# Top k of the first four units inside the weight rounding, first units no longer hurried, four chunks of 128 tokens, kept scores made in steps 4 to 11

## The chip, the cores and the metric

The kernel runs on one core of a Trainium2 chip. The metric is the device time of one execution in microseconds. Three runs of the kernel before gave 1446.69, 1447.28 and 1449.47 us; the median is 1447.28 us.

A core has a matrix engine (PE in the profile, with its weight loads as PEld), a vector engine (DVE), a scalar engine (ACT), GpSimd (POOL) and a queue engine (SP) that here issues nearly all DMA transfers. The program gives each its own list of instructions in a fixed order, with semaphore waits between the lists.

## The reference

Attention that keeps the 32 largest scores of each query, then a two-layer block with leaky ReLU. In NumPy, cut to what is computed:

```python
# q, k, v: (8 batches, 8 heads, 576, 64) float32
scores = 0.125 * q @ k.transpose(0, 1, 3, 2)
kth = np.partition(scores, -32, axis=-1)[..., -32:-31]
scores = np.where(scores >= kth, scores, -1e9)
attn = np.exp(scores - scores.max(-1)); attn /= attn.sum(-1) + 1e-9
x = (attn @ v).transpose(0, 2, 1, 3).reshape(4608, 512)
h = x @ w_in                       # w_in  (512, 2048)
out = np.maximum(0.01 * h, h) @ w_out   # w_out (2048, 512)
```

The two weights arrive as float64 (the scaling by `1/sqrt(...)` in the setup makes them so), and the kernel rounds them to float32 on the chip.

## The kernel before, in words

**Units and steps.** The heads are taken in pairs. A *unit* is 128 query rows of one head pair: a tile of scores of 128 x (2 x 576). There are 144 units, in the order batch, then block of 128 queries, then the four head pairs. One unit is one *step* of the main loop, which takes two steps per turn: `even(s)` (L801) and `odd(s)` (L858). A unit passes through:

- scores on PE (`scores`, L235), copied to `s_sb` by ACT (`keep_scores_of`, L244), two steps ahead of its own step;
- top k on DVE in its step (`top_k`): two `pairs` operations of max and min of the halves (L308), then four rounds of MAX8 (L314) and three of MATCH_REPLACE8 (L319) for each of the two heads;
- in the next step `limits` (ACT L329, POOL L330 and L331), `mask` (ACT L335), `exponents` (ACT L338) and `sums` (ACT L343, tile `ze`);
- `reciprocals` on DVE (L347, tile `rz` from `ze`), then `normalize` on ACT (L350);
- the transpose of the weights into `wT`. The usual way is `split` (two POOL copies L359, each written to DRAM from SP, L360) and `transpose` (a DMA transpose from SP, L364). For the units named in `HASTY` (L673) it is `transpose_in_haste` (PE L374) and `keep_transposed` (ACT L380), a step earlier;
- the product with v (`weigh_whole`, PE L403), copied into a chunk of `x` (`keep_values`, ACT L426). `values_at(n)` (L675) says at which step: three after the pair's second step, two for units in haste.

**The dense block.** Tokens are gathered into chunks (`CHUNKS`, L54), two of 128 and then 17 of 256. The first `EARLY` chunks go through `plain` (L629: `hidden_of_few`, PE L443 with ACT L438, transposes L460 with ACT L462, and PE L634); the others through `mlp` with a scheme of seven products (PE L542 and L556, ACT L530, sums on POOL in L481). `sum_weights` (L493) makes sums of the second weight on POOL, and `sum_last_weights` (L504) two more at the first chunk of the second kind. A chunk becomes ready when all its units are weighed (`ready_at`). Its matmuls are dealt out in slots, seven per step: `mlp_steps(budget)` issues matmuls until `budget` columns are used, and `slot_budget` (L701) gives `EARLY_SHARE` columns per slot while no more than `EARLY` chunks have become ready; later it spreads what is ready evenly up to the next chunk. Copies that follow a group of matmuls are put off to the next `catch_up()`.

**Kept scores.** The scores of twelve later units are made in the first steps (`score_early`, with the count per call from `EARLY_SCORES`, L682) by `keep_scores`: PE L288, ACT L292, then a DMA to DRAM (L294). They are fetched back before those units.

**The start.** Before the main loop the weights are loaded in 16 pieces of 1 MB and rounded in 17 jobs (the first piece in two halves). One job of `round_weights` is a POOL copy (L131), three short DVE operations (L132 to L134), three ACT operations (L135, L137, L139), six matmul steps (L149 to L151), and, after a `yield`, two DVE operations (L153, L156). The second part of a job is issued after the first part of the next one. The raw pieces use three buffers, so piece p is loaded into the buffer of piece p-3 when its job has read it (`load_weights`, L111). The main loop starts when the last job has been issued.

**Order.** All of this is an order written by hand; the tile framework adds the semaphore waits and the rotation of buffers (`bufs`), no reordering.

Of the kernel before, what the change touches and what calls it, by code (L numbers as in the profile page):

```python
# [16 lines left out]
NKC = 5  # L17
# [3 lines left out]
def kernel(  # L21
# [29 lines left out]
    WCH = 1024  # L51
    LEFT = S % P
    assert D == 64 and S == 576 and HP == 4 and B % 2 == 0 and LEFT == 64
    CHUNKS = [128] * 2 + [256] * 17  # L54
    assert sum(CHUNKS) == B * S
    CHMAX = max(CHUNKS)
    LOADED, LOADED_V = 7, 5
# [39 lines left out]
        return w_out[f // 4][:, f % 4:f % 4 + 2, :].rearrange("p g n -> p (g n)")  # L97

    raw_of = {}

    def load_weights(n):
        if n >= NPIECE:
# [12 lines left out]
    def round_weights(n, c0, c1):  # L115

        raw = raw_of[n][:, c0:c1, :]
        dst = piece(n)[:, c0:c1]
        wide = c1 - c0
        mid = raw[:, :, 2]
        low = raw_of[n].rearrange("p n w -> p (n w)").bitcast(U32).rearrange("p (n w) -> p n w", w=2)[:, c0:c1, 0]
        top = raws.tile([P, WCH], U16, name="top", bufs=2)[:, 0:wide]
        scale = raws.tile([P, WCH], U16, name="scale", bufs=2)[:, 0:wide]
        parts = work.tile([P, 2 * NKC - 1, P], F32, name="wT", bufs=3)
        parts = parts.rearrange("p c n -> p (c n)").bitcast(U16)
        m_top, m_low = parts[:, 0:wide], parts[:, WCH:WCH + wide].bitcast(BF16)  # L130
        nc.gpsimd.tensor_copy(top, raw[:, :, 3])  # L131
        nc.vector.tensor_scalar(scale, top, 4, 0x7FF, ALU.logical_shift_right, ALU.bitwise_and)  # L132
        nc.vector.tensor_scalar(m_top, top, 0xF, 0x3F80, ALU.bitwise_and, ALU.bitwise_or)
        nc.vector.tensor_scalar(top, top, 0x8000, None, ALU.bitwise_and)  # L134
        nc.scalar.activation(dst, mid, AF.Copy, bias=-7.0 - 2.0 ** -16, scale=2.0 ** -20)  # L135

        nc.scalar.activation(m_low, low, AF.Copy, bias=128.0, scale=2.0 ** -29)  # L137

        nc.scalar.activation(scale.bitcast(BF16), scale, AF.Exp, bias=least, scale=LN2)  # L139
        if n < NPIECE - 4 or n % 2 == 0:  # L140
            tag, bufs = ("wide", 2) if n < NPIECE - 4 else ("narrow", 1)
            pw = ps_sc.tile([P, 2, 512], F32, name=tag, bufs=bufs)
            sums = [(pw[:, c // 512, :], c) for c in range(0, wide, 512)]
            ends = [(pw.rearrange("p h n -> p (h n)")[:, 0:wide], 0)]
        else:
            ends = sums = [(ps_ml.tile([P, 512], F32, name="pw", tag="ml"), h * 512) for h in range(2)]
        for pw, c in sums:
            at = slice(c, c + 512)
            nc.tensor.matmul(pw, ident_top, m_top[:, at].bitcast(BF16), start=True, stop=False)  # L149
            nc.tensor.matmul(pw, ident, dst[:, at], start=False, stop=False)  # L150
            nc.tensor.matmul(pw, ident_low, m_low[:, at], start=False, stop=True)  # L151
        yield
        nc.vector.tensor_tensor(scale, scale, top, ALU.bitwise_or)  # L153
        for pw, c in ends:
            at = slice(c, c + pw.shape[-1])
            nc.vector.tensor_tensor(dst[:, at], pw, scale[:, at].bitcast(BF16), ALU.mult)  # L156
# [122 lines left out]
    def keep_scores(u):  # L279
# [5 lines left out]
        for half in range(2):  # L285
            for i, _, side, _ in u.parts:
                d = slice(side * D, (side + 1) * D)
                nc.tensor.matmul(ps[i][:, half, 0:HS], qt[d, :], kt[d, half * HS:(half + 1) * HS],  # L288
                                 start=True, stop=True)
        both = gT.rearrange("p f n -> p (f n)")[:, k % 3 * 2 * S:(k % 3 + 1) * 2 * S]  # L290
        for i in range(2):
            nc.scalar.copy(both[:, i * S:(i + 1) * S].rearrange("p (h n) -> p h n", h=2), ps[i][:, :, 0:HS])  # L292
        kept_of[u] = kept.tile([P, 2 * S], F32, name=f"kept{k}")
        nc.sync.dma_start(kept_of[u], both)  # L294

    def fetch_scores(u):
        u.both = work.tile([P, 2, S], F32, name="s_sb", bufs=5)
# [130 lines left out]
    QUARTERS = NKC  # L428
    FULL = list(range(NKC - 1))

    EARLY = 2

    def hidden_of_few(ch, x):

# [235 lines left out]

    HASTY = (*range(4), 14, 15, 142, 143)  # L673

    def values_at(n):  # L675

# [2 lines left out]
    steps = units  # L679

    KEPT = (26, 62, 98)
    EARLY_SCORES = {0: 4, 1: 2, 2: 2, 3: 2, 4: 2}  # L682

    def unit(n):
        return steps[n] if 0 <= n < len(steps) else None

    done_tokens, ready_at = [0] * len(CHUNKS), []
    for n, u in enumerate(steps):
        ch, _ = x_at(u.b * S + u.q0)
        done_tokens[ch] += u.rows * len(u.pairs)  # L690
        if done_tokens[ch] == CHUNKS[ch] * HP:
            ready_at.append(((values_at(n) | 1), ch))
    assert [ch for _, ch in ready_at] == list(range(len(CHUNKS)))

    def attended(s):
# [11 lines left out]
        group = [GROUP * (at % 2 == 0 and at < len(steps)) for at in range(s, until)]  # L707
        return max((backlog[0] + sum(group)) / len(group) - group[0], 0.0) / SLOTS

    EARLY_SHARE = 500  # L710
    GROUP = 1400
    SLOTS = 7

    with tc.manual_schedule():
# [39 lines left out]
                    break  # L754


        for n in range(3):
            load_weights(n)
        jobs = [round_weights(*job) for job in ROUNDED] if AS_WORDS else [iter(())] * len(ROUNDED)
        for n in range(len(jobs) + 1):  # L760
            if n == len(jobs) - 1:
                first = first_scores(steps[0])
                next(first, None)
            for job in jobs[max(n - 1, 0):n + 1][::-1]:
                next(job, None)
            if n == len(jobs) - 1:
                next(first, None)
                load_v(0)
                load_v(1)
            elif n == len(jobs):  # L770
                for _ in first_scores(steps[1]):
                    pass
            if n:
                load_weights(n + 2)
            if n >= len(jobs) - 2 and to_load:
                load_early(to_load.pop(0))
            if 0 <= n - len(jobs) + HP + 1 < HP:
                load_qk(n - len(jobs) + HP + 1)

        def values(s, spare):  # L780
            weighed = []
            for n in range(0, len(steps), 2):
                if values_at(n) != s:
                    continue
                us = steps[n:n + 2]
                po = spare.pop(0) if spare else ps_sc.tile([P, 2, 512], F32, name="wide", bufs=2)
                if len(us[0].pairs) == 1:
                    weigh_whole(us, po, FULL + [QUARTERS])
                    weighed.append((us[0], po[:, :, 0:P]))
                    continue  # L790
                for k, u in enumerate(us):
                    part = po[:, :, k * LEFT:(k + 1) * LEFT]
                    weigh_left(u, part)
                    weighed.append((u, part))
            return weighed

        def keep(weighed):
# [3 lines left out]
        def even(s):  # L801
# [28 lines left out]
            if old:  # L830
                exponents(old, 0)
                exponents(old, 1)
                sums(old)
            if older and in_haste:
                keep_transposed(older)
            if old:
# [6 lines left out]
                normalize(old, 0)  # L843
                normalize(old, 1)
            sum_now(2)
            score_early(EARLY_SCORES.get(s, 0))
            mlp_steps(budget)
            mlp_steps(budget)
            if unit(s + 3) in early_units:
# [8 lines left out]
        def odd(s, new, ps, weighed):  # L858
# [25 lines left out]
                keep(values(s, []))  # L884
            attended(s)
            budget = slot_budget(s)
            if s == 7:
                sum_weights()
            sum_now(3)
            mlp_steps(budget)  # L890
# [4 lines left out]
            if old and not in_haste:  # L895
                exponents(old, 1)
                sums(old)
            for _ in range(4):
                mlp_steps(budget)
            if unit(s + 3) in early_units:  # L900
                fetch_scores(unit(s + 3))
            score_early(EARLY_SCORES.get(s, 0))
            load_more(s)

        for s in range(0, len(steps) + 4, 2):
            assert s < 5 or not to_keep
            odd(s + 1, *even(s))
        mlp_steps(1e9)
        sum_now()
# [61 lines left out]
```

## Time and profile before

| | |
|---|---|
| median of three runs | 1447.28 us |
| the profiled execution: its time, and its span | 1447.51 us, 1445.7 us |
| DVE busy | 1318.6 us (91% of the span) |
| PE busy | 1363.7 us (94%) |
| ACT busy | 1028.6 us (71%) |
| POOL busy | 712.5 us (49%) |
| first `pairs` operation of unit 0, 4, 28 | 60.56, 95.79, 340.20 us |
| first `pairs` operation of the last unit, 143 | 1356.56 us |
| granted TensorE clock, mean | 0.976 |

How to read it: times are from the start of the profiled span. A row of a timeline or a group has line, engine, operation, output and inputs, shapes; "idle before" is time for which the engine stood still, with what ended it. The chain of waits follows the work back from the last instruction; idle time of an engine that is not on it costs nothing. The profiled execution's time is 1.8 us above its span (what lies around the program).

### The profile page before, as it was taken

How to read it: one execution, taken by the hardware profiler on the slowest of the kernel's cores; microseconds unless marked ns; L12 is line 12 of the kernel's file. 1: busy time of each engine (PE TensorE's matmuls, PEld its weight loads, DVE VectorE, ACT ScalarE, POOL GpSimd, SP SyncE). 2: the span in 40 equal slices, each digit the busy share in tenths (PEclk: the TensorE clock that was granted, in tenths of full speed). 3: DMA queues.
4: the chain of work that ended last, by engine and by line, in shares of the span. 5: the costliest groups of instructions: out<-in, count | busy, mean ns of one | idle time of the engine just before them, and what ended most of it. 6: DMA issues, size and time to landing. Idle time of an engine off the chain costs nothing.

```text
span 1445.7 us, 27893 instructions
## 1 busy us (share of the span) xinstructions
PE 1363.7 (94%) x9830; PEld 1066.7 (74%) x9832; DVE 1318.6 (91%) x3401; ACT 1028.6 (71%) x2151; POOL 712.5 (49%) x796
## 2 busy tenths in 40 slices
PE   7868887989999999999999999999999999999998
PEld 2344445767878888878888878888778888888887
DVE  7987998999999999999999999999999999999700
ACT  8877766767777777777777777767677777777621
POOL 3203630554646464656564555565555555555512
PEclk9968998999999999999999999999999999999999
DMA  8952542575666546665777556666765565655500
GB/s 332 344 184 83 131 125 79 158 195 151 184 178 181 161 134 187 194 183 131 206 181 192 148 139 184 196 177 145 203 187 166 139 158 150 169 139 139 127 12 15
DMA packets 389693, 234.55 MB, mean 162 GB/s; under 512 B 325680, under 2 KB 336432, under 8 KB 387632
## 3 DMA queue, kind: packets, MB, share of 16 engines
q1 hardware_dynamic: 388976, 232.24, 58.2%
q8 instruction: 77, 1.26, 0.4%
q14 instruction: 64, 0.52, 0.1%
q10 hardware_dynamic: 576, 0.52, 0.1%
HBM read 55.77 MB, written 96.73 MB: 105 GB/s over the span
## 4 chain that ended last, share of the span: by engine, by line
DVE 69%; PE 18%; issue 7%; ACT 4%; DMA 1%; POOL 1%; DVEq 0%; POOLq 0%; SPq 0%
DVE tops L314 33%; DVE pairs L319 25%; DVE pairs L308 7%; PE ph L542 6%; PE pz L556 6%; PE wide L403 3%; ACT s_sb L338 1%; DVE rz L347 1%; ACT s_sb L350 1%; PE wide L235 1%; DMA raw<-in_weights_dram 1%; PE wide L288 1%; DVE w_out L156 1%; ACT s_sb L244 1%; DVE scale L153 1%
## 5 line engine op out<-in xcount | busy, mean ns | idle before, releaser
L314 DVE MAX8 tops<-pairs 128x8 f32<-128x288 f32 (+1 forms) x1152 | 636.1, 592 | 0.0
L542 PE MATMUL ph<-x,w_in 128*128 128x256 f32 x2176 | 488.2, 383 | 7.1 <-ACT gT L530 6.8
L542 PEld LDWEIGHTS ph<-x,w_in 128*128 128x128 f32 x2176 | 409.2, 190 | 92.2 <-issue 16.1
L319 DVE MATCH_REPLACE8 pairs<-tops,pairs 128x288 f32<-128x288 f32 (+1 forms) x864 | 460.5, 539 | 0.0
L359 POOL COPY split<-s_sb 128x1152 uint16<-128x1152 uint16 x272 | 303.0, 1142 | 191.0 <-ACT s_sb L350 190.6
L350 ACT ACTIVATE s_sb<-s_sb,rz 128x576 f32<-128x576 f32 x288 | 206.9, 766 | 151.7 <-DVE rz L347 151.7
L330 POOL TENSOR_TENSOR nbias<-tops 128x2 f32<-128x2 f32 x144 | 73.1, 507 | 430.2 <-DVE tops L314 426.6
L556 PE MATMUL pz<-w_out,gT 128*128 128x256 f32 x1088 | 241.0, 379 | 2.2 <-ACT o_sb L564 1.7
L556 PEld LDWEIGHTS pz<-w_out,gT 128*128 128x128 f32 x1088 | 206.3, 190 | 31.9 <-POOL nbias L331 2.1
L308 DVE TENSOR_TENSOR pairs<-s_sb 128x576 f32<-128x576 f32 x288 | 215.5, 788 | 9.9 <-ACT nleast L329 0.5
L338 ACT ACTIVATE s_sb<-s_sb,nbias 128x576 f32<-128x576 f32 x288 | 223.5, 783 | 0.8 <-POOL nbias L331 0.8
L335 ACT ACTIVATE s_sb<-s_sb,nleast 128x576 f32<-128x576 f32 x288 | 207.6, 768 | 4.7
L403 PE MATMUL wide<-wT,vt 128*64 128x128 f32 (+1 forms) x2560 | 160.0, 287 | 15.3 <-ACT wT L380 9.3
L403 PEld LDWEIGHTS wide<-wT,vt 128*64 128x64 f32 (+1 forms) x2560 | 130.9, 140 | 51.7 <-issue 33.6
L556 PE MATMUL pz<-raw,top 128*128 128x256 f32 x544 | 124.4, 383 | 3.0 <-ACT o_sb L564 3.0
L556 PEld LDWEIGHTS pz<-raw,top 128*128 128x128 f32 x544 | 101.3, 190 | 26.0 <-issue 7.0
L530 ACT ACTIVATE gT<-ph 128x512 f32<-128x512 f32 x136 | 79.9, 588 | 35.6 <-PE ph L542 35.6
L235 PE MATMUL wide<-kt,qt 64*64 64x352 f32 x1040 | 103.8, 470 | 0.0
L244 ACT COPY s_sb<-wide 128x704 f32<-128x704 f32 x130 | 99.0, 762 | 0.2 <-PE wide L235 0.2
L329 ACT ACTIVATE nleast<-tops 128x2 f32<-128x2 f32 x144 | 28.6, 199 | 91.7 <-DVE tops L314 90.5
L564 ACT COPY o_sb<-pz 128x256 f32<-128x256 f32 x119 | 44.5, 374 | 65.2 <-PE pz L556 63.6
L331 POOL TENSOR_SCALAR nbias<-nbias 128x2 f32<-128x2 f32 x144 | 84.3, 586 | 12.6
(81 smaller groups left out, 1221.3 us busy)
## 6 DMA issues: line engine op xcount, KB each, us to landing
apart<-split SPq DMA_DIRECT2D x272, 288.0 KB, 2.4
raw<-in_weights_dram SPq DMA_DIRECT2D x15, 1024.0 KB, 7.0
vt<-in_vk_dram SPq DMA_DIRECT2D x32, 320.0 KB, 3.8
qt<-in_qT_dram SPq DMA_DIRECT2D x32, 288.0 KB, 3.6
kt<-in_kT_dram SPq DMA_DIRECT2D x32, 288.0 KB, 3.8
out_dram<-o_sb SPq DMA_DIRECT2D x68, 128.0 KB, 2.4
kept<-gT SPq DMA_DIRECT2D x12, 576.0 KB, 3.9
s_sb<-kept SPq DMA_DIRECT2D x12, 576.0 KB, 4.7
```

Source lines behind the costliest of these rows:

```text
L235: nc.tensor.matmul(to[r0:r0 + LEFT, i, :], qt[d, q0:q0 + LEFT], kt[d, k0:k1], start=True, stop=True)
L244: nc.scalar.copy(u.both[:, :, k0:k1], to)
L308: nc.vector.tensor_tensor(pairs[:, :, n, :], u.both[:, :, 0:HS], u.both[:, :, HS:S], op)
L314: nc.vector.max(out=u.tops[:, i, r, :], in_=rest[i])
L319: nc.vector.match_replace(out=rest[i], in_to_replace=u.tops[:, i, r, :], in_values=rest[i], imm_value=LOWEST)
L335: nc.scalar.activation(u.s[i], u.s[i], AF.Prelu, bias=u.nleast[:, i:i + 1], scale=1.0, alpha=BELOW)
L338: nc.scalar.activation(u.s[i], u.s[i], AF.Exp, bias=u.nbias[:, i:i + 1], scale=SCALE, accum_out=u.z[:, i:i + 1])
L350: nc.scalar.activation(u.s[i], u.s[i], AF.Copy, bias=0.0, scale=u.rz[:, i:i + 1])
L359: nc.gpsimd.tensor_copy(split, pairs[:, :, h])
L403: nc.tensor.matmul(po[n * D:(n + 1) * D, side, 0:P], v_of[u.pairs[0]][k, at, side, :], u.wT[k, at + side * NKC if at + 1 < NKC else at, :] ...
L542: nc.tensor.matmul(ph[:, i, 0:n], w_in[c][:, f * P:(f + 1) * P], x[:, c, 0:n], start=(c == 0), stop=(c == HP - 1),)
L556: nc.tensor.matmul(to, g[:, f, :], w(f), start=(first and f == 0), stop=(f == HALF - 1), skip_group_check=not first)
```

## The change

- `round_weights` takes its scratch `parts` from the `x` pool (two buffers) in place of `wT` (three), and puts its sums into the two single 512-column PSUM tiles `ml`, from the tenth piece on in turn with the tile `narrow`; before, the first twelve pieces used the two 1024-column tiles `wide`.
- A new `first_steps()` does the start: rounding, and steps 0 to 3 in between. Two calls of `round_more()` stand inside the top k of each of the first four units, and eight follow. These units are transposed by POOL copies and DMA, in `first_steps` too; the first four v tiles and the loads of q and k are spread over it. The main loop starts at step 4.
- `HASTY` keeps only units 142 and 143 (0 to 3, 14 and 15 leave it).
- Four chunks of 128 tokens and 16 of 256; `EARLY` is 4, `EARLY_SHARE` 560 (500 before). The first chunk is ready at step 3.
- Kept scores: one per step in steps 4 to 7, two per step in 8 to 11 (before: up to four per call at step 0 and two per call at steps 1 to 4, until the twelve were made). They pass through the two `top` buffers, each half with a DMA of its own, not through `gT`. One of two stands after `sums(old)`.
- `sum_weights` is asked for at step 13, not 7.

```diff
-    CHUNKS = [128] * 2 + [256] * 17
+    CHUNKS = [128] * 4 + [256] * 16
...
+    FIRST = 4
+    BESIDE = 2 * FIRST + 1
...
-        parts = work.tile([P, 2 * NKC - 1, P], F32, name="wT", bufs=3)
+        parts = xpool.tile([P, HP, CHMAX], F32, name="x")
...
-        if n < NPIECE - 4 or n % 2 == 0:
-            tag, bufs = ("wide", 2) if n < NPIECE - 4 else ("narrow", 1)
-            pw = ps_sc.tile([P, 2, 512], F32, name=tag, bufs=bufs)
+        if n >= BESIDE and n % 2 == 0:
+            pw = ps_sc.tile([P, 2, 512], F32, name="narrow")
...
-        both = gT.rearrange("p f n -> p (f n)")[:, k % 3 * 2 * S:(k % 3 + 1) * 2 * S]
+        kept_of[u] = kept.tile([P, 2 * S], F32, name=f"kept{k}")
         for i in range(2):
-            nc.scalar.copy(both[:, i * S:(i + 1) * S].rearrange("p (h n) -> p h n", h=2), ps[i][:, :, 0:HS])
-        kept_of[u] = kept.tile([P, 2 * S], F32, name=f"kept{k}")
-        nc.sync.dma_start(kept_of[u], both)
+            one = raws.tile([P, WCH], F32, name="top", bufs=2)[:, 0:S]
+            nc.scalar.copy(one.rearrange("p (h n) -> p h n", h=2), ps[i][:, :, 0:HS])
+            nc.sync.dma_start(kept_of[u][:, i * S:(i + 1) * S], one)
...
-    EARLY = 2
+    EARLY = 4
...
-    HASTY = (*range(4), 14, 15, 142, 143)
+    HASTY = (142, 143)
...
-    EARLY_SCORES = {0: 4, 1: 2, 2: 2, 3: 2, 4: 2}
+    EARLY_SCORES = {**{s: 1 for s in range(4, 8)}, **{s: 2 for s in range(8, 12)}}
...
-            ready_at.append(((values_at(n) | 1), ch))
+            ready_at.append(((values_at(n) | 1) if n >= FIRST else FIRST - 1, ch))
...
-    EARLY_SHARE = 500
+    EARLY_SHARE = 560
...
-        for n in range(3):
-            load_weights(n)
-        jobs = [round_weights(*job) for job in ROUNDED] if AS_WORDS else [iter(())] * len(ROUNDED)
-        for n in range(len(jobs) + 1):
...
+            score_early(EARLY_SCORES.get(s, 0) - 1)
...
-            score_early(EARLY_SCORES.get(s, 0))
+            score_early(int(s in EARLY_SCORES))
...
-            if s == 7:
+            if s == 13:
                 sum_weights()
...
+        def round_more():
+
+            n = begun[0]
+            begun[0] += 1
+            for job in jobs[max(n - 1, 0):n + 1][::-1]:
+                next(job, None)
+            if n:
+                load_weights(n + 2)
+            if n >= len(jobs) - 2 and to_load:
+                load_early(to_load.pop(0))
+
+        def first_steps():
+
+            load_weights(0)
+            load_qk(0)
+            load_weights(1)
+            load_qk(1)
+            load_weights(2)
+            load_qk(2)
+            load_qk(3)
+            round_more()
+            first = first_scores(steps[0])
+            next(first, None)
+            next(first, None)
+            round_more()
+            first = first_scores(steps[1])
+            next(first, None)
+            new = ps = None
+            for s in range(FIRST):
+                cur, old, older = steps[s], steps[s - 1] if s else None, steps[s - 2] if s > 1 else None
+                picks = top_k(cur)
+                if old:
+                    limits(old)
+                    mask(old, 0)
+                    mask(old, 1)
+                next(picks, None)
+                next(picks, None)
+                if s == 0:
+                    next(first, None)
+                elif s % 2:
+                    keep_scores_of(new, ps)
+                round_more()
+                if older:
+                    split(older)
+                    transpose(older)
+                if old:
+                    exponents(old, 0)
+                    exponents(old, 1)
+                    sums(old)
+                for _ in range(3):
+                    next(picks, None)
+                round_more()
+                if old:
+                    reciprocals(old)
+                    normalize(old, 0)
+                    normalize(old, 1)
+                for _ in picks:
+                    pass
+                load_v(s)
+                if s % 2 == 0:
+                    new = steps[s + 2:s + 4]
+                    ps, _ = tiles_for_scores(new)
+                    scores(new, ps)
+                    load_qk(s + 4)
+                    if s + 5 < LOADED:
+                        load_qk(s + 5)
+            a, b = steps[FIRST - 2:FIRST]
+            limits(b)
+            mask(b, 0)
+            mask(b, 1)
+            round_more()
+            split(a)
+            transpose(a)
+            exponents(b, 0)
+            exponents(b, 1)
+            sums(b)
+            round_more()
+            round_more()
+            reciprocals(b)
+            normalize(b, 0)
+            normalize(b, 1)
+            split(b)
+            transpose(b)
+            weighed = weigh(steps[0:2], ps_sc.tile([P, 2, 512], F32, name="wide", bufs=2))
+            while begun[0] <= len(jobs):
+                round_more()
+            weighed += weigh(steps[2:4], ps_sc.tile([P, 2, 512], F32, name="wide", bufs=2))
+            keep(weighed)
+            attended(FIRST - 1)
+            load_more(FIRST - 1)
+            return new, ps
+
+        first_steps()
+        for s in range(FIRST, len(steps) + 4, 2):
+            assert s < 12 or not to_keep
             odd(s + 1, *even(s))
```

`weigh(us, po)` is the inner part of the old `values`, under a name of its own.

More of the change, by code (lines that the diff above doesn't have):

```diff
@@ L145, in round_weights @@
         else:
-            ends = sums = [(ps_ml.tile([P, 512], F32, name="pw", tag="ml"), h * 512) for h in range(2)]
+            ends = sums = [(ps_ml.tile([P, 512], F32, name="pw", tag="ml"), c) for c in range(0, wide, 512)]
         for pw, c in sums:
@@ L681 @@
     KEPT = (26, 62, 98)
-    EARLY_SCORES = {0: 4, 1: 2, 2: 2, 3: 2, 4: 2}
+    EARLY_SCORES = {**{s: 1 for s in range(4, 8)}, **{s: 2 for s in range(8, 12)}}
     def unit(n):
-        return steps[n] if 0 <= n < len(steps) else None
+        return steps[n] if FIRST <= n < len(steps) else None
     done_tokens, ready_at = [0] * len(CHUNKS), []
@@ L754, in load_more, with weigh @@
                     break
-        for n in range(3):
-            load_weights(n)
-        jobs = [round_weights(*job) for job in ROUNDED] if AS_WORDS else [iter(())] * len(ROUNDED)
-        for n in range(len(jobs) + 1):
[L761 to L778, printed above, removed]
+        def weigh(us, po):
+            if len(us[0].pairs) == 1:
+                weigh_whole(us, po, FULL + [QUARTERS])
+                return [(us[0], po[:, :, 0:P])]
+            weighed = []
+            for k, u in enumerate(us):
+                part = po[:, :, k * LEFT:(k + 1) * LEFT]
+                weigh_left(u, part)
+                weighed.append((u, part))
+            return weighed
         def values(s, spare):
             weighed = []
-            for n in range(0, len(steps), 2):
+            for n in range(FIRST, len(steps), 2):
                 if values_at(n) != s:
@@ L786, in values @@
                 po = spare.pop(0) if spare else ps_sc.tile([P, 2, 512], F32, name="wide", bufs=2)
[L787 to L794, printed above, removed]
+                weighed += weigh(us, po)
             return weighed
@@ L897, in odd @@
                 sums(old)
+            score_early(EARLY_SCORES.get(s, 0) - 1)
             for _ in range(4):
@@ L901, in odd @@
                 fetch_scores(unit(s + 3))
-            score_early(EARLY_SCORES.get(s, 0))
+            score_early(int(s in EARLY_SCORES))
             load_more(s)
-        for s in range(0, len(steps) + 4, 2):
-            assert s < 5 or not to_keep
+        jobs = [round_weights(*job) for job in ROUNDED] if AS_WORDS else [iter(())] * len(ROUNDED)
+        begun = [0]
+        def round_more():
[7 more added lines that the diff above has]
+                load_early(to_load.pop(0))
```

## The prediction

> **What bounds the kernel now.** I read the chain of waits on the page first, then a table of stages cut at DVE's first `pairs` operation of units 0, 4 and 28 (60.56, 95.79, 340.20 us) and at the end of the last top k, then DVE's waits and the timeline around each.
>
> ```profile
> DVE 69%; PE 18%; issue 7%; ACT 4%; DMA 1%; POOL 1%; DVEq 0%; POOLq 0%; SPq 0%
> ```
>
> The end hangs on DVE, so the stages are read by DVE (columns: length, then busy time of PE, PEld, DVE, ACT, POOL, clock, DMA share, GB/s):
>
> ```profile
> 0.00:60.56 60.56, 47.59 (x142) 19.69 (x145) 49.26 (x90) 53.78 (x54) 19.26 (x24) 1.00 0.92 335
> 60.56:95.79 35.23, 25.00 (x148) 13.73 (x145) 34.88 (x92) 28.84 (x57) 2.96 (x7) 0.75 0.76 273
> 95.79:340.20 244.41, 205.25 (x1415) 135.46 (x1416) 217.75 (x553) 166.15 (x353) 101.52 (x107) 0.90 0.46 128
> 340.20:1366.54 1026.34, 1013.36 (x7730) 835.23 (x7729) 1016.53 (x2669) 762.14 (x1652) 570.20 (x640) 1.00 0.63 167
> 1366.54:1445.70 79.16, 72.46 (x400) 62.55 (x398) 0.17 (x1) 17.68 (x37) 18.55 (x20) 0.99 0.09 22
> ```
>
> From 340 us DVE is 99% busy: two units take 8.86 + 8.78 us, 8.82 each. That stage and the tail of 79 us (PE and the last sums; the last chunk and units 142, 143 are untouched) stay as they are. What can change lies before unit 28. Units 4 to 27 take 244.4 us where 24 x 8.82 = 211.7 would do: 32.7 too many. DVE's waits there, in total, number of times, longest:
>
> ```profile
> DVE rz L347 <- ACT ze L343: 25.1, 6, 8.0
> ```
>
> All six are reciprocals waiting for the sums of a unit in haste or beside one (ACT held up behind PE). The three longest, and what the rest is made of:
>
> ```profile
> 109.96 0.17 DVE L347 RECIPROCAL rz<-ze 128x2 f32<-128x2 f32 x1 [6.74 <-ACT ze L343]
> 134.73 0.17 DVE L347 RECIPROCAL rz<-ze 128x2 f32<-128x2 f32 x1 [6.12 <-ACT ze L343]
> 256.09 0.17 DVE L347 RECIPROCAL rz<-ze 128x2 f32<-128x2 f32 x1 [8.03 <-ACT ze L343]
> ```
> ```profile
> 142.33 4.80 POOL L481 TENSOR_TENSOR raw<-w_out,raw 128x1024 f32<-128x1024 f32 x2
> 145.03 3.39 DVE L308 TENSOR_TENSOR pairs<-s_sb 128x576 f32<-128x576 f32 x2
> ```
>
> The `pairs` operations, usually 1.43 us for two, take 3.39 beside POOL's sums of weights and end just after them. Units 8, 9 and 19 (unit 8: 145.03 to 155.83) are 2.0, 1.9 and 3.3 us longer than 8.82: 7.1 us. 25.1 + 7.1 is the excess within 0.5.
>
> Last, the rounding. Its pace is ACT's: three operations per job, end to end.
>
> ```profile
> 37.40 1.15 ACT L135 ACTIVATE w_out<-raw 128x1024 f32<-128x1024 uint16 x1
> 38.45 1.13 ACT L137 ACTIVATE wT<-raw 128x1024 bf16<-128x1024 uint32 x1
> 39.60 1.15 ACT L139 ACTIVATE scale<-scale,least 128x1024 bf16<-128x1024 uint16 x1
> 40.66 1.14 ACT L135 ACTIVATE w_out<-raw 128x1024 f32<-128x1024 uint16 x1
> ```
>
> A job takes 3.26 us (37.40 to 40.66). DVE needs 1.14 of it for the first part and 1.97 for the second, so it is nearly full too; the overlap the change makes has little idle time to fill: 60.56 - 49.26 = 11.3 us, most of it ahead of 12.7 us.
>
> **The change, part by part.**
>
> *When does unit 4 start?* Unit 0's scores now stand behind job 0 on PE (its matmuls end at 8.84); eight matmuls at about 0.2 and two copies (1.17 together) bring its top k to 11.4 us. From there DVE must do, before unit 3's top k ends: 4 x 8.78 = 35.1; first parts of eight jobs, 8 x 1.14 = 9.1; second parts of half a job and seven, 1.1 + 7 x 1.97 = 14.9; three reciprocals 0.2. That is 70.7 us. In this stretch every job's matmuls use the one pair of 512-column tiles. Between two second parts DVE has 4.4 of top k and 1.14 of a first part, 5.5 us, and a job's matmuls take 2.6 us at full clock, 5.0 at half (6.12 to 8.84 is one half job, cold). They fit, except at the two jobs where the scores of a next pair stand before them on PE: 0 or 2.5 us each. The clock row that is nearest is that of busy but broken PE work:
>
> ```profile
> 76.00:80.00 4.00, 2.58 (x8) 1.18 (x6) 3.90 (x8) 2.74 (x8) 0.79 (x2) 0.50 1.00 316
> 84.00:88.00 4.00, 4.00 (x14) 1.98 (x14) 3.97 (x10) 3.73 (x9) 0.86 (x2) 0.50 0.14 55
> 88.00:92.00 4.00, 3.58 (x38) 1.63 (x36) 4.00 (x14) 3.53 (x7) 0.50 (x1) 0.95 0.66 267
> ```
>
> The clock is 0.50 with PE busy 2.58 of 4 us, and 0.95 after a full slice. A job of 5.0 us is such a full slice, so I take one of the two waits, 2.5: unit 3 ends at 73.2.
>
> Eight calls of rounding are left, seven whole jobs and a last second part, and ACT has all of it in order: mask of unit 3 1.65, seven jobs 22.8, exponents and sum 1.8, normalize 1.4, then DVE's last second part 2.0: 29.7 us. On POOL the copies of four of these jobs stand behind unit 3's `split` (two of 1.14), which waits for that normalize: 2.3 more. Unit 4 starts at 73.2 + 32.0 = 105.2, against 95.79: **+9.4**. Bounds: +4.6 without the waits, +15 with both PE waits and a late weight load of 3.
>
> *The waits removed:* **-25.1**. Units 0 to 3, 14 and 15 no longer send ACT through PE transposes and early products. DMA transposes cost no DVE time (units from 20 on use them at 8.82); for units 0 to 3 their 4.7 us to landing are covered by the rest of the rounding. SP carries them ahead of weight pieces 9 to 15; this is a rival below. The 7.1 us beside POOL's sums stay: the same sums run, at step 13 and at chunk 4. If none coincides with a `pairs` operation, 7.1 go too.
>
> *New waits in steps 4 to 24.* PE per step: 3920 columns of a plain chunk (7.0 us: a chunk of 17,408 columns is 14.3 for the first layer, 14.3 for the second, 2.5 for transposes, warm), scores 0.97, a kept unit 2.0. Steps 4 to 7 ask 9.97 us where DVE takes 8.82, so PE falls 1.15 behind per step, from about 1 us at the start (the first x is copied when the last job has left PE and ACT). `reciprocals(old)` stands 7.3 us into an even step; ACT's mask, normalize and exponents need 5.0 of that, so 2.3 us of PE lag are free. At step 6 the lag is 3.3, at step 8 it is 5.6 less what step 6 waited: waits of 1 and about 3. Kept units in steps 8 to 11 fall where chunk 0 has run out (17,408 / 3920 = 4.4 steps) and chunk 1 isn't ready before 11. From 11 to 24 PE needs 7.0 + 0.97 + 1.14 (product with v) = 9.1: 3.8 us of lag in 13 steps, 2 of it felt. Together **+6**; bounds 0 and 13 (two waits like those of 6.74 and 6.12 above). The 256-token chunk becomes two plain ones: 62 us of PE for 53, the same lag, counted. By step 27 the early chunks are done in both orders, and what follows is equal.
>
> Nothing else is on the path: the kept scores' halves use the same DMA bytes, and the halved L156 costs 0.06 us a job.
>
> **Sum:** 9.4 - 25.1 + 6 = -9.7. The profiled execution took 1447.51 us (span 1445.7 and 1.8 around it), 0.2 above the median of 1447.28. Predicted: 1438.
>
> **Two rules of the Trainium skill, weighed.** SBUF — State Buffer, "Who interferes with whom", says that a DVE operation with two SBUF inputs, or in a two-port mode, and a GpSimd one that reads SBUF exclude each other, and whoever comes first keeps the ports. The 3.39 us row agrees. The rule speaks against the change: eight `split` copies now fall beside rounding's short DVE operations. If a third of their 9.1 us met one, the sum would be -6.7; the rows of units from 20 on, with two splits each and 8.82 us, give 0. TensorE: Matmul & The Clock Gate, "Part 1: The HAM clock gate", says that an idle window of about 3.4 us halves the clock and a busy one restores it. By it every rounding job with a gap starts cold and both waits of 2.5 count: -7.2 rather than -9.7.
>
> **The rivals.**
> - *The start packs tightly.* No PE wait, no POOL wait, step 4 to 24 as smooth as later steps: +4.6 - 25.1 = -20.5, 1427; without collisions down to 1423. For it: DVE's list leaves 5.5 us per job. Against it: PE's load of 9.97 per step.
> - *The waits come back under other names.* +9.4 and 13 to 16 of new reciprocal waits at steps 6 to 10: about 1447, no change. For it: the same ACT-behind-PE chain. Against it: no product in haste, the exponents now stand ahead of the kept copies.
> - *The weight loads come late: slower.* SP has the last pieces behind unit 3's split and transpose. A piece goes out when the job three before has read its buffer, 7.6 us ahead of its use (3 x 3.26 - 2.2); the page has 7.0 us to landing. If the last four loads slip, each slip is paid on ACT in full. At 2.5 us each the gain is gone; at 3.7 (7.0 - 3.26, no overlap) it is +15 and the time 1453. Against it: DMA is less loaded there than in the first 60 us, where it sustained a piece in 3.26.
> - *The removed waits were covered, and nothing moves:* hardly, as DVE leads the chain and has no idle time later to give back; what chance it has is in the 0.10 below.
>
> **How the numbers follow.** Change within 0.2% (2.9 us) can't be told from none. Chances: forecast 0.50 (own range 1431 to 1444), tight 0.27, waits back 0.10, late loads 0.13. Faster 0.77, same 0.10, slower 0.13. The range takes in the tight case and the waits that come back: 1424 to 1450, leaving late loads and the far tail of the tight case out.
>
> **What would show it.** Unit 4's first `pairs` at 105 us (100 to 111); 8.82 per unit right after; no reciprocal wait over 4 us before unit 28; unit 28 at 331 (340.2 before); 3.3 us `pairs` rows moved to units 13 to 15 and about 28. A unit 4 past 115, or reciprocal waits of 13 us in total, proves me wrong; so does a tail other than 79 us.

## The result and the profile after

The changed kernel takes 1473.62 us (median; 1469.88 to 1474.26) against 1448.38 us for the kernel before in the same session: **1.017 of it, 95% interval 1.0149 to 1.0191**. It is 25.2 us slower, where 9.7 us less were forecast, and it lies outside the range.

The profiled execution took 1473.06 us, its span is 1471.3. The profile page's line of the chain of waits, by engine:

```profile
DVE 60%; PE 25%; issue 6%; ACT 5%; DMA 2%; POOL 1%; SPq 1%; DVEq 0%; POOLq 0%; ACTq 0%
```

DVE carried 69% of the chain before and carries 60% now: there are stretches in which something else holds the end. The table of stages says where. It is cut at DVE's first `pairs` operation of unit 0, at the end of unit 3's top k, at the first `pairs` of units 4 and 28, and at the end of the last top k (columns: length, busy time of PE, PEld, DVE, ACT, POOL, clock, DMA share, GB/s):

```profile
0.00:12.04 12.04, 5.48 (x13) 2.16 (x13) 2.97 (x10) 4.33 (x7) 3.19 (x10) 1.00 0.85 327
12.04:74.24 62.20, 37.63 (x133) 15.06 (x136) 60.99 (x138) 46.70 (x67) 16.43 (x17) 0.80 0.68 233
74.24:114.92 40.68, 30.07 (x115) 13.39 (x115) 25.29 (x45) 27.54 (x33) 12.70 (x13) 0.81 0.88 270
114.92:362.12 247.20, 203.43 (x1312) 110.29 (x1309) 215.12 (x551) 166.79 (x351) 87.94 (x97) 0.92 0.57 158
362.12:1392.23 1030.11, 1013.65 (x7734) 836.64 (x7733) 1019.53 (x2669) 762.75 (x1652) 574.36 (x640) 1.00 0.62 166
1392.23:1471.30 79.07, 72.46 (x400) 62.54 (x398) 0.17 (x1) 17.69 (x37) 18.57 (x20) 0.98 0.08 21
```

The 25.6 us between the two profiled executions are in three places. Unit 4 starts at 114.92, not 95.79: 19.1. Units 4 to 27 take 247.20, not 244.41: 2.8, although the hurried units and their 25.1 us of waits are gone. From unit 28 to the end of the last top k it is 1030.11, not 1026.34: 3.8. The last stage is as long as it was (79.07, before 79.16). So the removed waits were replaced in units 4 to 27, and the start is twice as late as forecast. First the waits of DVE there (114.92 to 362.12: total, times, longest):

```profile
DVE rz L348 <- ACT ze L344: 22.7, 10, 5.6
DVE pairs L309 <- ACT s_sb L245: 8.1, 3, 5.2
```

The reciprocals wait for ACT again, and now the scores that ACT copies come late as well. What ACT itself waits for between 114.92 and 235 us:

```profile
ACT top L294 <- PE wide L289: 11.9, 4, 4.7
ACT top L294 <- DMA kept<-top: 11.7, 3, 6.0
ACT scale L439 <- PE ph L444: 5.9, 4, 3.2
ACT x L427 <- PE wide L404: 5.4, 1, 5.4
ACT x L427 <- PE wide L236: 5.3, 2, 3.0
ACT top L294 <- PE narrow L289: 4.5, 1, 4.5
```

Three of the six, 28.1 of 44.7 us, are one line, L294: the copy of a kept score into a `top` buffer. 16.4 us of it wait for the kept matmuls on PE, 11.7 for a buffer whose transfer to DRAM hasn't landed. The chain of waits, cut to the same stretch, shows one such wait link by link (links under 0.1 us left out):

```profile
163.42 2.24 POOL split L360 x2
165.69 2.11 DMA apart<-split
167.87 2.22 SPq L365
170.18 2.88 DMA kept<-top
173.15 0.65 ACT top L294
```

Read it downward. A unit's `split` is written to DRAM; SP's transpose of it (L365) waits for that write to land and starts at 167.87; the kept score's transfer stands behind the transpose in SP's order and is issued at 170.18; it lands near 173.1; only then does ACT copy the next half. ACT's own list says what stood behind it:

```profile
167.69 1.44 ACT L351 ACTIVATE s_sb<-s_sb,rz 128x576 f32<-128x576 f32 x2 [0.41 <-DVE pairs L309]
173.15 1.33 ACT L294 COPY top<-wide 128x576 f32<-128x576 f32 x2 [4.01 <-DMA kept<-top]
174.37 0.21 ACT L330 ACTIVATE nleast<-tops 128x2 f32<-128x2 f32 x1
174.61 1.44 ACT L336 ACTIVATE s_sb<-s_sb,nleast 128x576 f32<-128x576 f32 x2
```

The limits (L330) and mask (L336) of the next unit begin 4.01 us late, for scores of units from 26 on.

Now the start. Unit 3's top k ends at 74.24 (forecast 73.2). The rest of the rounding then takes 40.7 us, not 32.0. ACT, which sets its pace, has four waits in it:

```profile
85.76 1.13 ACT L139 ACTIVATE x<-raw 128x1024 bf16<-128x1024 uint32 x1 [0.81 <-PE pw L152]
90.04 1.44 ACT L351 ACTIVATE s_sb<-s_sb,rz 128x576 f32<-128x576 f32 x2 [1.87 <-DVE rz L348]
95.37 1.15 ACT L141 ACTIVATE scale<-scale,least 128x1024 bf16<-128x1024 uint16 x1 [1.75 <-DVE scale L134]
107.80 1.12 ACT L137 ACTIVATE w_out<-raw 128x1024 f32<-128x1024 uint16 x1 [4.64 <-DMA raw<-in_weights_dram]
```

Together 9.1 us. The largest is the last weight piece. SP's list from 89 us on:

```profile
89.11 1.04 SPq L113 DMA_DIRECT2D raw<-in_weights_dram  x2
92.78 1.43 SPq L361 DMA_DIRECT2D apart<-split  x2
100.06 2.18 SPq L365 DMA_TRANSPOSE wT<-apart  x1
102.33 0.53 SPq L113 DMA_DIRECT2D raw<-in_weights_dram  x1
```

Unit 3's two writes (92.78) were issued after two 1 MB weight loads (89.11), its transpose waits for them to land and starts at 100.06, some 6 us after their issue, and the last weight piece, which comes after it in SP's order, goes out at 102.33 and is used at 107.80. The 1.75 us come from POOL, in the same way: a job's copy (L133) has to wait for unit 3's `split` (L360), which waits for unit 3's normalize:

```profile
91.60 2.24 POOL L360 COPY split<-s_sb 128x1152 uint16<-128x1152 uint16 x2 [7.51 <-ACT s_sb L351]
93.79 1.09 POOL L133 COPY top<-raw 128x1024 uint16<-128x1024 uint16 x1
```

### The profile page after: what moved, and what is told of

Read it like the earlier page. It is cut to its first block, busy times and chain, and to the rows that moved or that the text cites. A ratio compares the mean times of both kernels' runs of the same rounds, so it can differ in the third digit from the quotient of the medians.

```text
span 1471.3 us, 27662 instructions
## 1 busy us (share of the span) xinstructions
PE 1362.7 (93%) x9695; PEld 1040.1 (71%) x9698; DVE 1324.1 (90%) x3411; ACT 1025.8 (70%) x2144; POOL 713.2 (48%) x796
## 4 chain that ended last, share of the span: by engine, by line
DVE 60%; PE 25%; issue 6%; ACT 5%; DMA 2%; POOL 1%; SPq 1%; DVEq 0%; POOLq 0%; ACTq 0%
DVE tops L315 28%; DVE pairs L320 22%; DVE pairs L309 6%; PE ph L543 5%; PE pz L557 5%; PE pz L635 3%; PE ph L444 3%; PE wide L404 3%; PE wide L236 1%; DMA apart<-split 1%; ACT s_sb L351 1%; PE narrow L236 1%; ACT s_sb L339 1%; DVE rz L348 1%; ACT s_sb L336 1%
## 5 line engine op out<-in xcount | busy, mean ns | idle before, releaser
L543 PE MATMUL ph<-x,w_in 128*128 128x256 f32 x2048 | 457.0, 382 | 6.9 <-ACT gT L531 6.0
L543 PEld LDWEIGHTS ph<-x,w_in 128*128 128x128 f32 x2048 | 384.5, 190 | 84.4 <-issue 16.3
L360 POOL COPY split<-s_sb 128x1152 uint16<-128x1152 uint16 x284 | 317.6, 1147 | 233.5 <-ACT s_sb L351 231.9
L557 PE MATMUL pz<-w_out,gT 128*128 128x256 f32 x1024 | 226.7, 379 | 0.6 <-POOL gT L482 0.6
L557 PEld LDWEIGHTS pz<-w_out,gT 128*128 128x128 f32 x1024 | 194.3, 190 | 27.8 <-POOL gT L482 1.4
L336 ACT ACTIVATE s_sb<-s_sb,nleast 128x576 f32<-128x576 f32 x288 | 207.9, 769 | 4.7
L404 PE MATMUL wide<-wT,vt 128*64 128x128 f32 (+1 forms) x2560 | 158.3, 287 | 24.7 <-DMA wT<-apart 16.8
L557 PE MATMUL pz<-raw,top 128*128 128x256 f32 x512 | 116.8, 383 | 3.9 <-ACT o_sb L565 3.9
L557 PEld LDWEIGHTS pz<-raw,top 128*128 128x128 f32 x512 | 95.4, 190 | 25.6 <-issue 6.2
L531 ACT ACTIVATE gT<-ph 128x512 f32<-128x512 f32 x128 | 75.3, 588 | 31.6 <-PE ph L543 31.5
L330 ACT ACTIVATE nleast<-tops 128x2 f32<-128x2 f32 x144 | 28.8, 200 | 79.6 <-DVE tops L315 78.9
```

The costliest lines, as they stand in the source:

```text
L336: nc.scalar.activation(u.s[i], u.s[i], AF.Prelu, bias=u.nleast[:, i:i + 1], scale=1.0, alpha=BELOW)
L360: nc.gpsimd.tensor_copy(split, pairs[:, :, h])
L404: nc.tensor.matmul(po[n * D:(n + 1) * D, side, 0:P], v_of[u.pairs[0]][k, at, side, :], u.wT[k, at + side * NKC if at + 1 < NKC else at, :] ...
L543: nc.tensor.matmul(ph[:, i, 0:n], w_in[c][:, f * P:(f + 1) * P], x[:, c, 0:n], start=(c == 0), stop=(c == HP - 1),)
L557: nc.tensor.matmul(to, g[:, f, :], w(f), start=(first and f == 0), stop=(f == HALF - 1), skip_group_check=not first)
```

## The experiments

The theories at the outset: the kept scores cost the time (through their transfers, or through PE, which also has the first chunks); the first chunks' share of PE per slot is too high; the start is late for one wait in SP's or POOL's order; and, the forecast's own, the removed haste is worth about 25 us. "Before" in each line is the kernel before in the same session.

### Four single edits (first session, before 1447.24 us)

**The kept transfers issued from ACT, not from SP** (on the changed kernel):

```diff
-            nc.sync.dma_start(kept_of[u][:, i * S:(i + 1) * S], one)
+            nc.scalar.dma_start(kept_of[u][:, i * S:(i + 1) * S], one)
```

> Edit: the 24 transfers of kept scores are issued from ACT's queue right behind their copy, not from SP. Theory Q (kept transfers stand in SP's queue behind DMA transposes that wait for their input, ACT then waits for one of the two top buffers: 11.7 us of ACT waits at three places, and PE behind them): those waits go, units 4 to 27 take about 235 us instead of 247.2, the kernel about 1461 us. Theory P (PE is given more per step than a step has, so ACT's copies and exponents come late): at most 3 us of change, since ACT gains 24 issues of 0.4 us; 1470 to 1476 us.

1473.58 us (1472.61 to 1475.73), ratio 1.0181 [1.0161, 1.0202]: no gain. ACT's waits in the same stretch (114.92 to 235):

```profile
ACT top L294 <- PE wide L289: 10.5, 4, 4.5
...
ACT top L294 <- ACT top L294: 4.9, 10, 0.7
ACT top L294 <- PE narrow L289: 4.8, 2, 4.5
...
ACT top L294 <- DMA kept<-top: 3.7, 3, 2.1
```

The wait for the transfers fell from 11.7 to 3.7 us, so SP's order was most of that wait. But ACT now waits for its own copy before it can issue (4.9), and the waits for kept matmuls stay (15.3, in the changed kernel 16.4). Units 4 to 27 take 247.4: 8 us less of waiting for transfers saved nothing, since other waits took its place.

**One more call of rounding ahead of unit 3's `split`:**

```diff
             normalize(b, 1)
+            round_more()
             split(b)
```

> Edit: one more rounding job is issued ahead of unit 3's split and transpose. Theory T (in the tail of the rounding the POOL copy of a job stands behind the split, and the last weight piece stands on SP behind the transpose, which waits 5.9 us for its input): the DVE waits of 4.9 and 4.3 us shrink, unit 4 starts near 108 us instead of 114.9, and the kernel takes about 1467 us. Rival (chunk 0 is what steps 4 on wait for, and it comes later by the same edit): unit 4 earlier, but units 4 to 27 longer by as much, total unchanged within 3 us.

1465.95 us (1465.52 to 1467.50), ratio 1.0128 [1.0109, 1.0148]: 7.7 us less than the changed kernel. Unit 4 starts at 108.94, 6.0 earlier. ACT's wait for the last weight piece falls from 4.64 to 1.6, and the one behind POOL's copy from 1.75 to 0.3. The two together (this run doesn't part them) were worth most of the gap between 40.7 and 32.0.

**A smaller share of PE for the first chunks:**

```diff
-            return EARLY_SHARE * (0.6 if s - 2 in HASTY else 1.0)
+            return 400 if s < 11 else EARLY_SHARE
```

> Edit: 400 columns per slot in steps below 11 (560 after). Theory P: PE has 8.0 us of work in steps 4 to 7 instead of 10.0, the reciprocal waits of units 6 and 8 (3.2 and 4.4 us) go; about 1467 us, with some of it back in steps 8 to 10, where chunk 0 now lasts to step 10. Theory Q: those waits stay, 1472 to 1476 us.

1469.41 us (1468.62 to 1471.28), ratio 1.0153 [1.0129, 1.0176]. Units 6 and 8 are 1.3 and 1.0 us over 8.82 (3.3 and 4.5 in the changed kernel), but unit 10 is 7.9 over, not 4.3. The share shifts the wait more than it removes it.

**The kernel before, without haste, and nothing else:**

```diff
-    HASTY = (*range(4), 14, 15, 142, 143)
+    HASTY = (142, 143)
```

> Edit: the kernel before, with only units 142 and 143 in haste; nothing else. If the haste of units 0 to 3, 14 and 15 by itself cost the 25.1 us of reciprocal waits, this takes about 1430 us, less 0 to 8 for a later first chunk: 1425 to 1438. If the waits come from ACT and PE being loaded with kept scores and the first chunks at the same time, they stay under other names: 1443 to 1452.

**1424.40 us** (1423.17 to 1424.97), ratio 0.9838 [0.982, 0.9857]. Its waits of DVE between 60 and 380 us:

```profile
DVE rz L347 <- ACT ze L343: 4.7, 4, 2.1
DVE pairs L308 <- ACT s_sb L244: 0.3, 1, 0.3
```

25.1 us of reciprocal waits became 4.7; units 4 to 27 take 221.35 us, not 244.41. This one line beats both kernels by a wide margin. So one part of the change is worth 23 us, and the others together cost about 49.

### Which of the others (second session, before 1448.07 us)

**The changed kernel without kept scores** (the twelve units are scored at their own time):

```diff
-    KEPT = (26, 62, 98)
+    KEPT = ()
```

> Edit: the changed kernel with no unit on the list of kept scores; the twelve units are scored in their own steps like all others. Theory K (making kept scores in steps 4 to 11, while PE has the first chunks, is what makes units 4 to 27 take 247 us): they take about 228 us; the kernel 1455 to 1465 us, since twelve units' scores come back into steps where PE is 98% busy. Theory C (the two further plain chunks do it): units 4 to 27 stay above 240 us.

1444.42 us (1442.73 to 1446.52), ratio 0.9977 [0.9967, 0.9987]: 29.2 us less than the changed kernel. Reciprocal waits from 60 to 380 us:

```profile
DVE rz L348 <- ACT ze L344: 4.7, 4, 2.1
```

Units 4 to 13 run at 8.81 each (115.28 to 203.36, ten units), with the same plain chunks at the same share. The start is unchanged (unit 4 at 115.28). The time expected, 1455 to 1465 us, allowed for the twelve units' own scores at a busy PE; that price did not show: from unit 28's first `pairs` operation to unit 143's it is 1018.52 us, in the changed kernel 1020.13.

**Four chunks of 128 tokens, on the kernel without haste:**

```diff
-    CHUNKS = [128] * 2 + [256] * 17
+    CHUNKS = [128] * 4 + [256] * 16
...
-    EARLY = 2
+    EARLY = 4
...
-    EARLY_SHARE = 500
+    EARLY_SHARE = 560
```

> Edit: the kernel before without haste (1424.4 us), and four chunks of 128 with their share of 560 columns; nothing else of the change. Theory K: at most 4 us more, 1424 to 1429. Theory C: 15 us more or worse, 1440 and up.

1431.62 us (1430.02 to 1433.90), ratio 0.9889 [0.9874, 0.9905]: 7.2 us more than without haste alone. Between the two profiled executions it is 5.7 us: 1.4 in units 4 to 27 (222.75), the rest later. The 1.3 us that unit 29 is over 8.82 are not new: its `pairs` operations take 2.81 us beside POOL's sums of weights, and without the further chunks the same 2.81 us stood at unit 21. So 2.7 us are new in units 4 to 27, and 2.4 at units 96 and 97.

**The kept scores in steps 4 to 11 through the two `top` buffers, on the kernel without haste:**

```diff
-    EARLY_SCORES = {0: 4, 1: 2, 2: 2, 3: 2, 4: 2}
+    EARLY_SCORES = {**{s: 1 for s in range(4, 8)}, **{s: 2 for s in range(8, 12)}}
...
+        for i in range(2):
+            one = raws.tile([P, WCH], F32, name="top", bufs=2)[:, 0:S]
...
-            if s == 7:
+            if s == 13:
```

> Edit: the kernel before without haste (1424.4 us), and the kept scores made in steps 4 to 11 through the two top buffers, with the sums of weights at step 13; nothing else of the change. Theory K: units 4 to 27 go from 221 to about 240 us, the kernel to about 1440. Theory C: at most 4 us more, 1424 to 1429.

1452.62 us (1451.75 to 1455.10), ratio 1.0038 [1.0025, 1.0051]: **28.2 us more**, which is more than the removed haste gave. DVE's waits from 60 to 380 us:

```profile
DVE rz L347 <- ACT ze L343: 20.6, 5, 6.5
DVE pairs L308 <- ACT s_sb L244: 12.2, 2, 8.3
```

The waits of the changed kernel are back without the new start and without the new chunks. Moving the kept scores costs 28.2 here; taking them out of the changed kernel altogether (the run before the last) gave 29.2.

**Three calls of rounding per unit in the first four, not two** (on the changed kernel):

```diff
-    BESIDE = 2 * FIRST + 1
+    BESIDE = 3 * FIRST + 1
...
+                round_more()
...
-            round_more()
```

> Edit: the changed kernel with three rounding jobs inside each of the first four units, so that four calls are left behind unit 3 instead of eight. Theory T (behind unit 3's top k the rest of the rounding runs at ACT's pace while DVE idles 15 of 41 us): the tail of 40.7 us shrinks to about 25, units 0 to 3 grow by 4 x 3.1 us, unit 4 starts at 108 to 112 us instead of 114.9, the kernel takes 1466 to 1471 us. Rival (the interleaving itself makes the rounding slow, wherever the jobs stand): units 0 to 3 grow by 5 us each or more, unit 4 not before 115.

1472.64 us (1470.11 to 1473.39), ratio 1.0168 [1.0152, 1.0184]: no gain, though unit 4 starts at 107.28, 7.6 earlier. ACT's waits from 100 to 235 us:

```profile
ACT x L427 <- PE wide L404: 12.9, 1, 12.9
ACT top L294 <- PE wide L289: 11.9, 4, 4.7
ACT top L294 <- DMA kept<-top: 11.4, 3, 5.4
```

The first product with v now lies in the steps, where ACT waits 12.9 us for it, and units 5 and 6 are 3.1 and 8.3 over 8.82. The time gained at the start was given back at once.

### What it is about the kept scores (third and fourth session, before 1447.93 and 1448.42 us)

Two candidates: PE, where kept matmuls stand behind the first chunks' (theory P), and the two half-buffers with two transfers per unit (theory B).

**Kept scores in steps 3 to 8, before any chunk begins** (on the kernel without haste and with kept scores through `top`):

```diff
-    EARLY_SCORES = {**{s: 1 for s in range(4, 8)}, **{s: 2 for s in range(8, 12)}}
+    EARLY_SCORES = {s: 2 for s in range(3, 9)}
...
-            ready_at.append(((values_at(n) | 1), ch))
+            ready_at.append((max(values_at(n) | 1, 9), ch))
```

> Edit: the kernel of the kept-later run (no haste, kept scores through the two top buffers, 1452.6 us), but with two kept units in each of steps 3 to 8 and the first chunk not ready before step 9, so that no kept unit stands behind matmuls of a chunk on PE. The transfers stand on SP among DMA transposes as before. Theory P (a kept copy makes ACT wait until PE has gone through the chunk's matmuls of that step, and the unit's mask and exponents behind it come late): waits of DVE before unit 13 fall from 33 us to under 6, the kernel takes 1424 to 1430 us. Theory Q (two buffers and SP's queue): the waits of 8 us stay, 1445 us or more.

1448.38 us (1446.01 to 1449.33), ratio 1.0001 [0.9992, 1.001]. With no chunk on PE the waits for kept matmuls are gone from ACT's list (90 to 200 us), but the others have grown:

```profile
ACT top L293 <- DMA kept<-top: 28.7, 7, 7.6
ACT x L426 <- PE wide L235: 5.6, 2, 2.9
```

No chunk on PE is needed for a loss of this size.

**The same through the three slots of `gT`, one transfer per unit, as before the change:**

```diff
-            one = raws.tile([P, WCH], F32, name="top", bufs=2)[:, 0:S]
-            nc.scalar.copy(one.rearrange("p (h n) -> p h n", h=2), ps[i][:, :, 0:HS])
-            nc.sync.dma_start(kept_of[u][:, i * S:(i + 1) * S], one)
+            nc.scalar.copy(both[:, i * S:(i + 1) * S].rearrange("p (h n) -> p h n", h=2), ps[i][:, :, 0:HS])
+        nc.sync.dma_start(kept_of[u], both)
```

> Edit: as the run with the kept scores in steps 3 to 8 and the first chunk held to step 9 (1448.4 us; ACT waits 28.7 us there for a top buffer that its transfer still reads), but the kept scores pass through the three slots of gT with one transfer per unit, as in the kernel before. Steps, DMA transposes and SP's order stay. Theory B (two half buffers, each free only when its transfer has left SP and landed, are too few): the 28.7 us go, the kernel takes 1424 to 1430 us. Theory S (transfers of kept scores between DMA transposes on SP stall ACT whatever the buffer): 1440 us or more.

1425.86 us (1425.33 to 1426.88), ratio 0.9849 [0.9833, 0.9866]: 22.5 us less. ACT's waits at L292, the copy's line here (90 to 200 us), and DVE's wait (60 to 380 us):

```profile
ACT gT L292 <- PE wide L288: 1.5, 3, 0.9
ACT gT L292 <- PE narrow L288: 1.2, 2, 0.9
```
```profile
DVE rz L347 <- ACT ze L343: 2.2, 2, 1.7
```

No wait for a kept transfer is left. The bytes are the same; the staging (six half slots, not two, and half as many transfers) is the whole difference. Which of the two counts, the slots or the number of transfers, no run parts.

**One kept unit per step in steps 4 to 15** (on the changed kernel, so with chunks and with the two buffers):

```diff
-    EARLY_SCORES = {**{s: 1 for s in range(4, 8)}, **{s: 2 for s in range(8, 12)}}
+    EARLY_SCORES = {s: 1 for s in range(4, 16)}
...
-            if s == 13:
+            if s == 17:
```

> Edit: the changed kernel (1473.6 us) with one kept unit per step in steps 4 to 15 and the sums of weights at step 17. Theory B: the three ACT waits for a top buffer (11.7 us) go, as a pair of transfers has a whole step to land; units 4 to 27 fall from 247 to about 235 us, the kernel to 1459 to 1464 us. Theory P (ACT's kept copy waits for PE, which has the chunk's matmuls of the step in front): the 12 or so us of ACT waits for kept matmuls stay or grow, since more kept units now meet a chunk on PE; both may hold, and then 1460 to 1468 us.

1462.88 us (1461.80 to 1464.66), ratio 1.0104 [1.0089, 1.0119]: 10.7 us less than the changed kernel, 18.5 more than without kept scores. ACT's waits (114 to 250 us) hold no transfer now, only PE:

```profile
ACT top L294 <- PE wide L289: 14.2, 5, 4.7
ACT top L294 <- PE narrow L289: 7.6, 2, 4.5
```

So theory B is shown where there is no chunk: the staging alone costs 22.5 us. With chunks, and with the buffers' waits gone, 18.5 us of the kept scores' price are left. The trace points to PE (21.8 us of ACT's waits above), but that is argued, not shown: the 24 copies' own time on ACT is in the 18.5 as well, and no run has chunks and kept scores through the three slots of `gT` in these steps.

**Four chunks and no kept scores, on the kernel without haste:**

```diff
-    KEPT = (26, 62, 98)
+    KEPT = ()
```

> Edit: the kernel before without haste, with four chunks of 128 and no kept scores; it differs from the changed kernel without kept scores (1444.4 us) by the start alone. If the interleaved start costs what unit 4's start shows (115.3 against 96.1 us), this takes 1425 us; if steps 4 to 27 give some of it back, 1430 to 1436; if the start costs nothing in the end, 1444.

1427.62 us (1426.65 to 1428.05), ratio 0.9853 [0.9836, 0.9869]. It differs from the changed kernel without kept scores (1444.42) by the new start (and, with it, the sums of weights at step 7, not 13): that start costs 16.8 us. Unit 4 begins at 95.72 here and at 115.28 there, 19.6 later; units 4 to 27 give 2.6 of it back (222.30 against 219.75).

### The sum

| step from the one above | us | difference |
|---|---|---|
| before | 1447.2 | |
| haste removed | 1424.4 | -22.8 |
| four chunks of 128 | 1431.6 | +7.2 |
| kept scores as before, taken out | 1427.6 | -4.0 |
| rounding with units 0 to 3 inside it | 1444.4 | +16.8 |
| kept scores in steps 4 to 11, through `top` | 1473.6 | +29.2 |

The sessions' times of the kernel before differ by up to 1.2 us, so no difference here is better than that. Whoever leaves kept scores where they were pays 4.0 for them; moving them cost 25.2 on this path, 28.2 on the kernel without haste.

## Why the prediction was wrong

In the forecast's own terms, the sum -25.1 + 9.4 + 6 measured -22.8 + 16.8 + 32.4. The last is 7.2 for the chunks and 25.2 for the moved kept scores, and it is most of the miss.

**The step that failed first: "Nothing else is on the path: the kept scores' halves use the same DMA bytes."** The bytes are the same. What changed is the staging: two halves where there were three units, twice as many transfers, and a place in SP's order behind transposes that wait for their own input. ACT works through its list in order, so its wait of 4.01 us before 173.15 holds the next unit's limits and mask as well. In the sum this is a term of zero; alone it measures 22.5 us where there is no chunk. In the changed kernel it is 11.7 us of ACT's time; with one kept unit per step that wait was gone and the kernel 10.7 us shorter, while issuing from ACT saved nothing.

**The new waits in steps 4 to 24, +6 with bounds 0 and 13.** Units 4 to 27 took 247.20 us, and 221.35 with only the haste removed: 25.9 more. The forecast priced a kept unit as 2.0 us of PE and let a lag of 1.15 us per step build up. Without kept units its own terms leave none in steps 4 to 7 (7.0 + 0.97 is under 8.82), and none was seen: 8.81 per unit in steps 4 to 13. What the 2.0 leaves out is the place: the kept matmuls stand behind the chunk's on PE, the copies stand in ACT's order ahead of the next unit's mask, and a copy then waits up to 4.7 us. How the 25.2 us divide between this and the buffers stays open. The forecast held against the rival of returning waits that "the exponents now stand ahead of the kept copies". They do, but the last copies of a step stand ahead of the next unit's limits and mask, as the row at 173.15 shows. By mechanism that rival came nearest: reciprocal waits of 22.7 us, far over the 13 that were to prove the forecast wrong. With 8.1 at `pairs` it was larger than its own price of 13 to 16.

**"Unit 4 starts at 73.2 + 32.0."** The first part came out within 1.0 us (74.24), partly by luck. It held 2.5 us for a PE wait, and no wait of DVE for PE shows between 12.04 and 74.24. In its place unit 0 began at 12.04, not 11.4 (the forecast's own terms, 8.84 + 8 x 0.2 + 1.17, give 11.6), and DVE was busy 60.99 us where the list has 59.3. Among these are 3.1 us lost beside POOL's copies (last section), which the sum had at nothing. The second part was 8.7 short. ACT waited 9.1 us where 2.3 had been put down for POOL (1.8 were seen), and from ACT's last rounding operation, which ends at 110.98, to unit 4 it took 3.9 us, not 2.0. The late weight load, a rival that needed "the last four loads", happened for one piece (4.64) and for the reason given there, SP's order behind unit 3's split and transpose. Unit 4's start is 19.1 later than before, 4.1 over the upper bound of 15; the new start costs 16.8 of the final time.

**"The same lag, counted", of the plain chunks.** They cost 7.2 us. Part of it, 2.4 us, is at units 96 and 97, where the forecast had "what follows is equal". The run with four chunks and no kept scores does not show these 2.4; why they are there stays open.

**What was right.** The removed haste: 25.1 forecast, 22.8 measured alone. The last stage: 79. The `pairs` operations that are slow beside POOL's sums moved to units 14, 15 and 29 (4.16, 2.98 and 2.82 us), as forecast (13 to 15 and about 28). And the remark that DVE has little idle time in the rounding to fill: 11.3 us, against which stood a later start for each of the 140 units behind.

**The rules.** The Trainium skill's page TensorE: Matmul & The Clock Gate, "Part 1: The HAM clock gate", led to both PE waits of 2.5 and a sum of -7.2. The clock was indeed low in that stretch, 0.80 from 12.04 to 74.24, but neither wait came: DVE's own list filled 60.99 of the 62.20 us. In the rest of the rounding, at 0.81, ACT waited 0.81 us for PE and DVE 3.4, DVE being busy for only 25.29 of 40.68 us. The port lock of SBUF — State Buffer, "Who interferes with whom", fits what the last section shows: 4.9 us, 3.1 of them where DVE's list is full. The forecast had 3.0 by the rule and took 0 from the rows of units from 20 on, which hold none of these short operations.

## What to carry to other kernels

When work is moved to another place, list what stands behind each of its instructions on every engine that runs in order, the DMA queue included; bytes and busy time tell nothing of that. Count how many buffers its transfers may occupy, and take for each the time from the copy to the landing with its turn in the queue, not the transfer time. And price the parts of a change one by one: the one line that paid here (22.8 us) was outweighed by parts that had been priced at 15 and cost 49.

## What the runs showed that was not expected

The profile gives a kept transfer 2.3 us from issue to landing (median of 24), yet ACT waited up to 7.6 us for one in the run with kept scores before the chunks: a transfer's turn in SP's order isn't in that number.

```profile
kept<-top SPq DMA_DIRECT2D x24, 288.0 KB, 2.3
```

The Trainium skill's page DMA: Bandwidth & Descriptors, "Anatomy of one DMA — SWDGE (gpsimd) path", says of DMA engines in general that any semaphore wait happens on the issuing sequencer before dispatch. The runs fit that: issued from ACT, where no transpose's wait stands ahead of them, the same transfers cost ACT 3.7 us of waiting for a buffer, not 11.7.

DVE's short operations in the rounding also meet POOL's copies. Two of them at 75.9 us, while POOL copied until 78.26, took three times as long as the third, which came after:

```profile
75.82 2.44 POOL L360 COPY split<-s_sb 128x1152 uint16<-128x1152 uint16 x2
```
```profile
75.91 1.34 DVE L134 TENSOR_SCALAR scale<-top 128x1024 uint16<-128x1024 uint16 x1 [1.67 <-POOL top L133]
77.17 1.36 DVE L135 TENSOR_SCALAR x<-top 128x1024 uint16<-128x1024 uint16 x1
78.57 0.43 DVE L136 TENSOR_SCALAR top<-top 128x1024 uint16<-128x1024 uint16 x1
```

It happens at each of the three jobs whose operations fall beside a `split` copy: those at 44.08 and at 60.64 took 1.01 and 1.36 us, beside copies from 43.65 to 46.09 and from 60.20 to 62.65. In every other whole job the two take 0.42 or 0.43 each. The three pairs cost 4.9 us (2.37, 2.37 and 2.70 for 0.85 each), where the forecast had 3.0 by the rule and 0 by its rows.

These operations have one SBUF input; by the SBUF page's section such an operation can only meet GpSimd in a two-port mode, which fits, though no run here shows the mode.
